# Retention and a GELU block on one Trainium2 core: the first block's second product by half-size products, and another order of loads

## The chip, the core and the metric

The kernel runs on one core of a Trainium2 chip. The core has a matrix engine (TensorE, "PE" in the profile; its weight loads are listed as PEld), a vector engine (VectorE, DVE), an engine for activation functions (ScalarE, ACT), a general engine (GpSimd, POOL) that here issues nearly all loads, and SyncE (SP), which here issues the stores. They run side by side, each its own instructions in order, and wait for each other by semaphores. On-chip data lies in SBUF; matrix products land in eight banks of PSUM.

The metric is the device time of one execution in microseconds. The kernel before took 288.04 us, the median of three runs (287.86 to 289.65).

## The reference

Inputs are q, k, v of shape (8, 8, 576, 64): 8 sequences, 8 heads, 576 positions, 64 features. The weights are w_in (512 x 2048) and w_out (2048 x 512).

```
gamma = 1.0 - 2.0 ** (-5.0 - arange(H))
Dmat  = where(rel >= 0, gamma ** rel, 0)        # rel = row position - column position
ret   = (scale * q @ k^T) * Dmat
x     = (ret @ v), heads put side by side        # (4608, 512)
h     = x @ w_in                                 # first product
out   = gelu_exact(h) @ w_out                    # second product, (4608, 512) float32
```

## The kernel before, in words

**Units, groups, blocks.** The 4608 rows are cut into 36 units of 128 tokens (a chunk of one sequence, or the 64-token tails of two). Units 0 to 3 are groups of their own; from unit 4 on a group is a pair of units (the same chunk of two sequences) or a tail. Four units make a block of 512 tokens, so there are nine blocks, t = 0 to 8. Group 4 (units 4, 5) and group 5 (units 6, 7) make block 1; groups 6 and 7 block 2.

**Attention of a group.** q and k are turned so that features lie on the partitions: by transposes on TensorE (`turn`, L515) for units 0 to 3 and for the groups in `BY_PE` (L73: groups 4 and 5), by block transposes on DVE (`turn_dve`, L541, with a rearranging copy on ACT, `apart`, L555) for all others. Then come the scores, a mask by DVE (`masked`), the products within the chunk (`inner`), the running state of a sequence pair (`state`, which for the DVE-turned groups needs k a second time in its natural order, the `kn_ld` load, item n in the list of loads) and the product with the state of the chunk before (`cross`). `evacuate` writes x to SBUF. Two neighbouring groups may be done in one go ("AA").

**The first product of a block** (`mlp1`, or `mlp1_fast` in the last blocks) multiplies x by w_in, 256 columns of w_in to a loaded chunk, in pieces of 128, 256 or 512 tokens, and ACT writes GELU of it to `g_all`. Block 0 is done chunk by chunk and unit by unit as both arrive. Block 1 is done by halves: units 4 and 5 for all chunks, then units 6 and 7.

**The second product** has two forms. The plain form (`mlp2`, L838) takes 16 matmuls of 512 columns for 128 tokens and needs of w_out only the rows that it multiplies. The form with seven half-size products (`mlp2_fast`, L904; a Strassen-Winograd scheme) does 256 tokens, p = 0 or 1, with 7 x 8 matmuls of 256 columns, instead of the 32 of 512 columns of the plain form for the same tokens. It needs sums of w_out, made once by DVE (`w_out_sums`, L861: eight instructions, in the order 1, 2, 4, 3, two each), and four sums of g per 256 tokens (`g_sum`, L875); partial results are copied out of PSUM (`snap`, by DVE or ACT) and joined by DVE (`join`, L900). The products are done in the order 1, 2, 6, 5, 7, 4, 3. Products 1 and 2 need w_out only, 6, 5, 7 and 4 its sums. `fast_ready` (L951) asks for all of w_out before any of them. Before the change blocks 1 to 8 use this form, and of block 0 the second half (p = 1); its first half is plain.

**What sets the order.** A planner in the kernel itself writes the instruction streams. It keeps an estimated time for each engine (`T`), picks for TensorE the next piece that is ready by the estimates, hands out DVE and ACT jobs in `side_jobs` and `fire`, and issues loads on POOL in the order of a list written by hand (`ORDER`, L376; items wi and wo are chunks of w_in and w_out, q, k, v and n those of a unit or pair, dq is a table, io the constants). On the chip each engine goes through its stream in that order. The constants at L85 to L104 steer the planner: AHEAD and RATE limit how far scores run ahead of the blocks, STATE10 holds back the first state of sequence pair 1, JOIN, VISIT, LEAD and NEAR decide when two groups are done in one go, SB how late DVE may be when scores are begun, PER_G and PER_B weigh DVE's jobs, MSK_AT says when the mask is due. The planner lets the sums of w_out start when by its estimate all of w_out has landed (L1233) and units 0 to 3 are through, as they use the space of those units' q and k. Block 2's first product may not begin before block 0's second is done, since they share `g_all`.

## Time and profile before

| | us |
|---|---|
| median of three runs | 288.04 |
| the profiled execution | 288.46 |
| its span (first to last instruction) | 286.7 |
| TensorE busy | 277.8 |
| DVE busy | 229.7 |
| ACT busy | 176.7 |
| POOL busy (issuing loads, mostly) | 141.0 |
| bytes moved by DMA | 31.97 MB |

The profile lists one execution. Busy time is the time in which an engine has an instruction running; matmuls overlap in the pipeline, so the time that a row of them takes is better read from the starts of one piece and the next. L450 is the line of a helper through which all matmuls go, and L454 of the one for transposes on TensorE, so pieces are told apart by their tiles: `x,w_in` is the first product, `w_out,g_all`, `wt,s`, `wt,g_all` and `w_out,s` the second, `q_ld,kT` the scores, `zeros` are dummy matmuls that only keep TensorE occupied. POOL's DMA instructions are the issuing; "to landing" counts from there to the arrival.

### The profile page before, as it was taken

The numbers are of one execution on the slowest core, as the hardware profiler recorded it, in microseconds if no ns is written. First come the engines' busy times: TensorE is split into PE (matmuls) and PEld (weight loads), VectorE is DVE, ScalarE is ACT, GpSimd is POOL, SyncE is SP. The second block draws the span as 40 slices with busy tenths as digits, with TensorE's granted clock in tenths as the row PEclk, the third lists the DMA queues.
The fourth block names the chain that finished last, engine by engine and source line by source line (L and its number), as shares of the span: only waits on it lengthen the run. The fifth ranks groups of instructions, "written<-read, shape, count | busy, mean of one in ns | idle before, by whom it ended". The sixth has DMA issues, their size and how long they took to land.

```text
span 286.7 us, 9851 instructions
## 1 busy us (share of the span) xinstructions
PE 277.8 (97%) x4216; PEld 210.3 (73%) x4216; DVE 229.7 (80%) x387; ACT 176.7 (62%) x403; POOL 141.0 (49%) x213
## 2 busy tenths in 40 slices
PE   7889998999999999999999999999999999999994
PEld 2568766888864657756676676677888888888883
DVE  6754586767995699898978599969999999999861
ACT  7456425876888895688587766764555363655421
POOL 8976898799959977778665864000000000000000
PEclk9999999999999999999999999999999999999999
DMA  9999999999999999999999996302020201202014
GB/s 158 176 179 188 195 152 173 188 132 143 128 154 108 116 167 120 205 146 135 142 150 160 101 139 54 71 2 75 2 75 0 77 4 72 75 0 75 37 57 129
DMA packets 109276, 31.97 MB, mean 112 GB/s; under 512 B 85936, under 2 KB 104880, under 8 KB 109232
## 3 DMA queue, kind: packets, MB, share of 16 engines
q0 software_dynamic: 100528, 21.12, 83.8%
q1 hardware_dynamic: 6752, 9.37, 9.9%
q10 hardware_dynamic: 1952, 0.85, 1.3%
q8 instruction: 33, 0.54, 0.8%
q14 instruction: 11, 0.09, 0.1%
HBM read 42.99 MB, written 9.44 MB: 183 GB/s over the span
## 4 chain that ended last, share of the span: by engine, by line
PE 61%; DMA 22%; POOL 12%; issue 2%; ACT 1%; DVE 0%; POOLq 0%
PE psum L450 60%; DMA kn_ld<-in_k_dram 6%; DMA w_out<-in_moe_w_out_dram 6%; DMA q_ld<-in_q_dram 5%; POOL k_ld L346 3%; POOL q_ld L346 2%; DMA v_ld<-in_v_dram 2%; DMA early<-in_q_dram 2%; POOL v_ld L357 2%; DMA k_ld<-in_k_dram 1%; POOL dqT L320 1%; PE psum L454 1%; POOL kn_ld L352 1%; POOL w_in L310 1%; POOL k_ld L336 1%
## 5 line engine op out<-in xcount | busy, mean ns | idle before, releaser
L450 PE MATMUL psum<-x,w_in 128*128 128x256 bf16 (+2 forms) x792 | 117.8, 295 | 0.6 <-DMA w_in<-in_moe_w_in_dram 0.6
L450 PEld LDWEIGHTS <-w_in 128*128 128x128 bf16 x792 | 69.0, 98 | 29.1 <-DMA w_in<-in_moe_w_in_dram 1.2
L450 PEld LDWEIGHTS <-g_all 128*128 128x128 bf16 x576 | 55.5, 98 | 13.5 <-issue 0.3
L450 PE MATMUL psum<-w_out,g_all 128*128 128x256 bf16 (+1 forms) x440 | 57.9, 280 | 0.0
L346 POOL DMA_DIRECT2D k_ld<-in_k_dram x64 | 35.5, 577 | 23.8 <-DMA kn_ld<-in_k_dram 14.1
L816 ACT ACTIVATE g_all<-psum 128x512 bf16<-128x512 f32 x64 | 36.9, 592 | 16.4 <-PE psum L450 14.8
L450 PEld LDWEIGHTS <-s 128*128 128x128 bf16 x408 | 39.5, 98 | 7.6 <-issue 0.6
L634 ACT ACTIVATE vh<-v_ld,dv 128x128 bf16<-128x128 bf16 (+1 forms) x144 | 42.1, 378 | 0.0
L617 DVE TENSOR_TENSOR ret<-psum,msk 128x1024 bf16<-128x1024 f32 (+1 forms) x32 | 35.5, 1149 | 6.3 <-PE psum L450 6.2
L1030 ACT ACTIVATE g_all<-t 128x512 bf16<-128x512 f32 x36 | 22.6, 630 | 28.2 <-DVE t L1038 28.2
L487 ACT COPY t<-psum 128x256 f32<-128x256 f32 (+1 forms) x48 | 20.7, 433 | 29.7 <-PE psum L450 29.5
L346 POOL DMA_DIRECT2D q_ld<-in_q_dram x64 | 35.6, 583 | 1.9 <-DMA k_ld<-in_k_dram 1.0
L450 PE MATMUL psum<-wt,s 128*128 128x256 bf16 x272 | 33.5, 273 | 0.3 <-ACT t L487 0.3
L901 DVE TENSOR_TENSOR o_sb<-psum,t 128x256 f32<-128x256 f32 x51 | 21.4, 420 | 13.1 <-PE psum L450 7.2
L1038 DVE TENSOR_TENSOR t<-psum,t 128x512 f32<-128x512 f32 x36 | 24.6, 687 | 2.7 <-ACT t L487 1.1
L819 ACT ACTIVATE g_all<-psum 128x256 bf16<-128x256 f32 (+1 forms) x43 | 19.5, 488 | 11.2 <-PE psum L450 10.6
L485 DVE COPY t<-psum 128x512 f32<-128x512 f32 (+1 forms) x39 | 21.6, 564 | 0.4 <-PE psum L450 0.3
L450 PE MATMUL psum<-x,ws 128*128 128x256 bf16 x144 | 19.5, 273 | 0.0
L450 PE MATMUL psum<-wt,g_all 128*128 128x256 bf16 x136 | 17.5, 273 | 0.0
L450 PE MATMUL psum<-w_out,s 128*128 128x256 bf16 x136 | 17.5, 273 | 0.0
L357 POOL DMA_DIRECT2D v_ld<-in_v_dram x14 | 16.5, 1180 | 1.0 <-ACT g_all L816 0.7
L785 DVE TENSOR_TENSOR x<-psum,dqT 128x1024 bf16<-128x1024 f32 (+1 forms) x14 | 15.5, 1137 | 0.1
(100 smaller groups left out, 326.2 us busy)
## 6 DMA issues: line engine op xcount, KB each, us to landing
out_dram<-o_sb SPq DMA_DIRECT2D x31, 256.0 KB, 3.3
q_ld<-in_q_dram POOLq DMA_DIRECT2D x56, 64.0 KB, 5.5
k_ld<-in_k_dram POOLq DMA_DIRECT2D x56, 64.0 KB, 4.7
v_ld<-in_v_dram POOLq DMA_DIRECT2D x14, 256.0 KB, 5.3
kn_ld<-in_k_dram POOLq DMA_DIRECT2D x12, 256.0 KB, 6.8
w_in<-in_moe_w_in_dram POOLq DMA_DIRECT2D x8, 256.0 KB, 8.4
w_out<-in_moe_w_out_dram POOLq DMA_DIRECT2D x8, 256.0 KB, 7.1
q_ld<-in_q_dram POOLq DMA_DIRECT2D x16, 32.0 KB, 4.5
```

The source lines that it names most:

```text
L346: nc.gpsimd.dma_start(qk["qk".index(what)][p0:p0 + 32, 0:HP * per].rearrange("p (h x) -> p h x", h=HP), {"q": q, "k": k}[what][2 * bp + jj ...
L357: nc.gpsimd.dma_start(v_ld.rearrange("p j h d -> p (j h) d"), v[2 * bp:2 * bp + 2, :, ci * C:ci * C + C, :].rearrange("b h s d -> s (b h) d"))
L450: nc.tensor.matmul(*a, **k)
L485: nc.vector.tensor_copy(dst, src)
L487: nc.scalar.copy(dst, src)
L617: nc.vector.tensor_tensor(both.rearrange("p (e h) s -> p e h s", e=2), t, by, op=ALU.mult)
L634: nc.scalar.activation(vh[:, 0:m, h], src[:, :, h], AF.Copy, scale=dv[:, h, ci:ci + 1])
L816: nc.scalar.activation(g_all[:, t % 2, :, m0, :], hT.rearrange("p n (a c) -> p (n a) c", a=2), AF.Gelu)
L819: nc.scalar.activation(g_of(t, 2 * lo // TOK)[:, m0:m0 + n, lo_:lo_ + hi - lo], hT, AF.Gelu)
L901: nc.vector.tensor_tensor(dst, src, f[key], op=ALU.add)
L1030: nc.scalar.activation(g_of(t, part)[:, m0:m0 + 2], src, AF.Gelu)
L1038: nc.vector.tensor_tensor(f[key], f["b"][1], f[key], op=ALU.add)
```

## The change

The second half of block 0 was already done by seven half-size products; now the first half is too, so no plain second product is left in the kernel. `sum_due`, the list of the sums of g, gets the four sums of block 0's first half. NPE goes from 2 to 1: group 5 is turned by DVE, as all groups behind it are, and therefore item n6 becomes a real load. The list of loads is reordered, and the planner's constants are set anew.

```diff
@@ -67,7 +67,7 @@
     PLAIN = 4
-    NPE = 2
+    NPE = 1
...
-    AHEAD = 35
-    RATE = 0.4
+    AHEAD = 27
+    RATE = 1.6
     STORE_AT = 62.0
     CROWD = 66.0
-    STATE10 = 28.0
+    STATE10 = -20.0
...
-    JOIN = 1
+    JOIN = 2
     JOIN_SB = 0.0
-    VISIT = 8
-    LEAD = -3.0
-    NEAR = 3.2
-    SLACK, SB, PER_G, PER_B, TURN0 = 1.2, 2.0, 8.0, 20.0, 0.0
+    VISIT = 6
+    LEAD = 5.0
+    NEAR = 1.4
+    SLACK = 1.2
+    SB = 2.6
+    PER_G = 6.0
+    PER_B = 20.0
+    TURN0 = 0.0
...
-    MSK_AT = -58.0
+    MSK_AT = -18.0
...
-    ORDER = ("wi4 io wo2 q2 q1 k1 k2 wi5 wi3 n4 v1 wi1 v2 wi0 wi2 k3 q3 v3 wi7 dq2 wi6 wo6 q4 wo4 q5 wo0 wo1 wo3 "
-             "wo5 k5 wo7 q6 k4 k7 v4 q7 k6 q8 v6 q12 dq0 q9 v12 k9 k13 q10 n8 k11 k8 v8 dq3 k10 q11 v10 k12 n10 "
-             "dq4 q13 n6 n12").split()
+    ORDER = ("wi5 io k1 q1 v2 v4 q3 v1 k3 q2 k2 v3 k4 wi1 q4 wi7 q5 wi0 wi2 k5 wi3 dq2 wi6 wo4 wi4 wo2 wo0 q6 wo3 "
+             "wo6 wo1 wo5 wo7 k6 n12 k8 v8 q7 q9 n4 n8 k7 k9 v6 dq3 n6 q10 k11 v12 k10 q8 q11 dq0 v10 dq4 q13 k12 "
+             "q12 k13 n10").split()
...
@@ -1102,8 +1106,8 @@
         elif t == 0:
-            runs2.append((t, [("2", t, ts, m, m + 2) for m in range(0, N_DF, 2) for ts in range(2)]))
-            runs2.append((t, [("f", t, 1, x) for x in "1265743"]))
+            for p in range(2):
+                runs2.append((t, [("f", t, p, x) for x in "1265743"]))
...
     for t in (0, *FAST2):
-        for p in range(2) if t else (1,):
+        for p in range(2):
             sum_due += [(t, p, i) for i in "1234"]
```

## The prediction

> **What bounds the kernel now.** I read the page first: its busy times, its slices and the shares of the chain of work that ended last.

> ```profile
> span 286.7 us, 9851 instructions
> PE 277.8 (97%) x4216; PEld 210.3 (73%) x4216; DVE 229.7 (80%) x387; ACT 176.7 (62%) x403; POOL 141.0 (49%) x213
> ...
> PEclk9999999999999999999999999999999999999999
> ...
> PE 61%; DMA 22%; POOL 12%; issue 2%; ACT 1%; DVE 0%; POOLq 0%
> ```

> TensorE is busy for 97% of the span, but a third of the chain is DMA and POOL. The view by stretches shows where, once without a filter (columns: stretch, its length, busy time and count per engine, granted clock, DMA share, GB/s) and once for the matmuls on the tile `zeros`, dummies that only keep TensorE occupied:

> ```profile
> 0.00:20.14 20.14, 16.57 (x209) 9.39 (x209) 14.28 (x47) 11.53 (x24) 17.05 (x26) 1.00 1.50 172
> 20.14:45.94 25.80, 24.71 (x337) 18.86 (x338) 15.33 (x24) 12.29 (x33) 21.33 (x29) 1.00 1.72 184
> 45.94:81.19 35.25, 35.19 (x744) 30.09 (x745) 27.21 (x36) 26.63 (x65) 30.34 (x46) 1.00 1.57 149
> 81.19:200.00 118.81, 118.43 (x2058) 78.10 (x2055) 98.62 (x141) 87.03 (x212) 72.28 (x113) 1.00 1.11 119
> 200.00:283.00 83.00, 82.94 (x873) 73.82 (x872) 73.84 (x142) 39.26 (x72) 0.00 (x0) 1.00 0.13 46
> ...
> 0.00:10.00 10.00, 6.30 (x17) 1.95 (x17) 0.27 (x1) 1.00 1.22 161
> 10.00:20.14 10.14, 2.34 (x7) 0.64 (x7) 0.00 (x0) 1.00 1.78 182
> ```

> From 45.94 us to 283 TensorE idles 0.06 + 0.38 + 0.06 = 0.5 us. So the end is fixed by two numbers: how much matmul work there is, and how much of the time before 45.94 is lost. Useful work by then is 16.57 + 24.71 - 6.30 - 2.34 = 32.6 us; **lost are 13.3 us**, 12.2 before 20.14 and 1.1 behind it. DVE is busy 83% (98.62 / 118.81) and 89% later on, close, but its waits end nothing there.

> **The change part by part.** First the matmul work, from the order of instructions on TensorE (start, duration, instruction; consecutive starts give the time a piece takes, since durations overlap):

> ```profile
> 33.01 8.12 PE L450 MATMUL psum<-w_out,g_all 128*128 128x512 bf16 x40
> 40.97 0.61 PE L454 MATMUL psum<-ident,k_ld 128*128 128x128 bf16 x8
> ...
> 45.94 0.61 PE L454 MATMUL psum<-ident,q_ld 128*128 128x128 bf16 x8 [1.08 <-DMA q_ld<-in_q_dram]
> 46.38 1.04 PE L450 MATMUL psum<-w_out,g_all 128*128 128x256 bf16 x8
> 47.47 0.61 PE L454 MATMUL psum<-ident,k_ld 128*128 128x128 bf16 x8
> 48.01 0.63 PE L450 MATMUL psum<-ret,vh 128*32 128x128 bf16 x32
> ...
> 49.17 1.05 PE L450 MATMUL psum<-wt,g_all 128*128 128x256 bf16 x8
> ...
> 56.35 7.16 PE L450 MATMUL psum<-x,w_in 128*128 128x256 bf16 x64
> 63.44 0.63 PE L450 MATMUL psum<-q_ld,kT 32*128 32x128 bf16 x32
> 64.00 3.67 PE L450 MATMUL psum<-x,w_in 128*128 128x256 bf16 x32
> ...
> 68.76 1.92 PE L450 MATMUL psum<-w_out,g_all 128*128 128x256 bf16 x16
> 70.52 1.91 PE L450 MATMUL psum<-wt,s 128*128 128x256 bf16 x16
> ```

> *Seven products.* Sixteen half-size matmuls take 70.52 - 68.76 = 1.76, 0.11 each. The piece from 33.01 to 40.97 is the plain product of the first token half, 32 matmuls of 512 columns, and eight half-size ones (merged in one row): 7.96 - 8 x 0.11 = 7.08 for the 32. In their place come 7 x 8 x 0.11 = 6.16. **Gain 0.92.**

> *One group fewer on TensorE.* Group 5 (units 6 and 7) loses its 16 transposes: 46.38 - 45.94 = 0.44 and 48.01 - 47.47 = 0.54. **Gain 0.98.** The 1.08 of waiting before 45.94 is for the same group's q; it goes too, and I count it with the lost time below.

> *What the other engines get.* These groups carry it (busy us, mean ns):

> ```profile
> L548 DVE STREAM_TRANSPOSE kT<-k_ld 128x512 f32<-128x512 f32 x12 | 13.4, 1114 | 0.0
> L559 ACT COPY q_ld<-qT 128x1024 bf16<-128x1024 bf16 x12 | 12.5, 1042 | 0.0
> L901 DVE TENSOR_TENSOR o_sb<-psum,t 128x256 f32<-128x256 f32 x51 | 21.4, 420 | 13.1 <-PE psum L450 7.2 <-ACT t L487 5.0 <-issue 0.2
> L883 DVE TENSOR_TENSOR s<-s,g_all 128x1024 bf16<-128x1024 bf16 x17 | 11.7, 688 | 0.4
> L485 DVE COPY q_ld<-psum 128x1024 bf16<-128x1024 bf16 x2 | 1.4, 690 | 2.4 <-PE psum L454 2.4
> ```

> DVE gains four sums (2.75), three joins (1.26) and two transposes (2.2), and loses one copy of 0.69: about 5.5 us. ACT gains a 1.04 copy; the short evacuations that it gains and loses roughly cancel. The cover on DVE is the 8.0 us in which it is free between 45.94 and 81.19 and the 10.5 before that. If that cover were gone the 5.5 us would meet a stage at 83% and be paid partly.

> *Loads.* The new order has group 5's natural-order k (item n6, no load before because the transposed tile served both uses), one more 256 KB transfer, with fourteen items of the list behind it: late enough to stand behind what TensorE needs first. More important is what moves ahead: group 4's q, k and v now precede most of w_in, and w_out comes last.

> ```profile
> 1.25 0.89 POOL L310 DMA_DIRECT2D w_in<-in_moe_w_in_dram  x1 [0.80 <-POOLq L1433]
> ...
> 31.13 0.73 POOL L325 DMA_DIRECT2D w_out<-in_moe_w_out_dram  x1
> ...
> w_in<-in_moe_w_in_dram POOLq DMA_DIRECT2D x1, 256.0 KB, 6.1
> ...
> w_out<-in_moe_w_out_dram POOLq DMA_DIRECT2D x1, 256.0 KB, 7.1
> ...
> L368 POOL DMA_DIRECT2D early<-in_q_dram x3 | 2.7, 892 | 0.2 <-issue 0.2
> L336 POOL DMA_DIRECT2D q_ld<-in_q_dram x8 | 6.1, 769 | 2.4 <-DMA w_in<-in_moe_w_in_dram 1.8 <-issue 0.6
> L357 POOL DMA_DIRECT2D v_ld<-in_v_dram x14 | 16.5, 1180 | 1.0 <-ACT g_all L816 0.7 <-issue 0.2
> ```

> The first chunk lands at 1.25 + 6.1 = 7.35, the last w_out chunk at 31.13 + 7.1 = 38.2. Between them land 15 chunks of 256 KB and 12 tiles of 128 KB, 5376 KB in 30.9 us: 174 KB/us. In the changed order POOL issues, ahead of the second w_in chunk, the first chunk (0.8), two iotas (0.45), nine tiles (9 x 0.9), v4 (1.18) and k4 (2 x 0.77): it starts at about 13.3 and lands 6 to 7 us later, at 20. From there to the last w_in chunk are 2176 KB, 12.5 us (32.5), to the last w_out chunk 4096 KB, 23.5 us (**43.5, where 38.2 was**).

> *Lost time.* By 20 us TensorE can have done the attention of units 0 to 3 and their work with one w_in chunk. That is one unit's attention more than before and w_in matmuls of one chunk instead of several, so about the 7.9 us of before (16.57 - 8.64); unit 3's v is among the last to land, so I take 7.4, an estimate that may be off by 0.7 either way: 12.6 lost. From 20 to 43.5 it has seven chunks of block 0's first product (16 matmuls of 256 columns each, 7.09 / 64 = 0.111 apiece: 12.4), group 4 (transposes 0.98 as above, scores 64.00 - 63.44 = 0.56, the rest 49.17 - 48.01 = 1.16: 2.7) and, new as cover, the first half of block 1's first product (64 matmuls, 7.1): 22.2 of work for 23.5. Then the first block's second product waits for the w_out chunks and for the DVE sums of w_out, which the replaced plain product did not:

> ```profile
> 36.17 1.28 DVE L870 TENSOR_TENSOR wt<-w_out 128x1024 bf16<-128x1024 bf16 x2
> ...
> 40.18 1.29 DVE L870 TENSOR_TENSOR w_out<-w_out 128x1024 bf16<-128x1024 bf16 x2
> ```

> All eight sums took 41.47 - 36.17 = 5.3; the first two read only the first half of w_out and began before the last chunk was there, at 36.17 against 38.2. So the last sums stand between 47.2 (begun early again) and 48.8 (begun at 43.5). Until then TensorE has 7.4 + 22.2 + four of the seven products (3.5) = 33.1 of work: lost 14.1 to 15.7. If the order is better than my count and only the wait before 45.94 goes, it is 12.2. I take 14.1, nearest to the row that shows the sums begun ahead of the last chunk: **0.8 more lost than before**. Behind the waiting matmul stands everything on TensorE, since it runs in order, and behind it the evacuations of block 0 and the first stores.

> *After that.* Group 5's v lands some 12 us behind the last w_out chunk by POOL's issue times, about 55 (ten loads at 1.18); the second product of block 0 (14 x 0.88 = 12.3) and the first half of block 1's (6.2) fill TensorE until about 62. No hole there.

> *The other constants.* MSK_AT is negative before and after, so the mask is due at once in both. The limits for scores ahead, the joining of two groups, the early state of pair 1 only reorder instructions in stretches where TensorE idles 0.5 us of 237: nothing can be gained, up to 1 us lost or some mode changes saved; I take 0, with 1 us to each side.

> *Sum.* -0.92 - 0.98 + 0.8 = -1.1. The profiled execution took 288.46, 1.76 more than its span and 0.4 over the median 288.04; span 285.6, execution 287.4, **287.0 at the median's level**.

> [...] The longest hole in which TensorE did nothing was 1.2 us, at the start, and the clock was granted at 1.00 in every stretch above:

> ```profile
> PE psum L450 <- DVE zeros L150: 1.2, 1, 1.2
> PE psum L454 <- DMA q_ld<-in_q_dram: 1.1, 1, 1.1
> ```

> [...]

> **The rivals.**

> 1. *The start gets tighter and nothing new waits.* For it: the wait for group 5's q is gone and work that needs no w_out is pulled ahead. Against: w_in's second chunk lands at 20, and 7.4 us of work before it isn't more than 7.9. Lost 12.2: -1.9 - 1.1 = **285.0**.

> 2. *The second product takes the place of the plain one as a wait (slower).* Its place is TensorE between the end of block 0's first product, near 35, and the sums of w_out near 47. What hides it is the 7.1 us of block 1, which needs q4, q5, k4, k5, two transposes, scores, mask, cross product and evacuation before it. Each us of that cover that comes too late is a us lost. With none of it 287.0 + 7.1 = 294.1, with half 290.6; over 290.9 (1% slower) from 3.9 us on. For it: the chain is DMA and POOL in that stretch, and a plain product that could start chunk by chunk is gone. Against: the last of group 4's loads, k5, is ahead of the last three w_in chunks. I price it at **291**.

> 3. *DVE becomes the bound* between 81 and 200, if its 5.5 us of new work and another order of its jobs push mask and evacuation late: **289.5**. Against: its 20 us of free time there.

> [...]

> That the seven products are not done as said can be excluded by the matmul counts; that the retuned constants change nothing cannot, and is within the forecast.

> **How the numbers follow.** Forecast 287.0, from 285.2 to 289 by the ends above (lost 13.3, as before, to 15.7, and some 0.7 us either way for the reordering): 0.52. Rival 1: 0.16. Rival 2: 0.24, two thirds of it above 290.9. Rival 3: 0.05. Rival 4: 0.03. A measurement of this kernel tells about 1%, 2.9 us, from no change: 0.15 faster (below 285.16), 0.20 slower, 0.65 within. The range, 284.8 to 291.8, reaches over rival 1's middle and into rival 2; about one in ten is left on each side.

> **What would show it.** The plain matmuls of 512 columns on w_out gone (32) and 56 half-size ones in their place; 16 transposes of L454 fewer; k by natural order 13 times instead of 12. The first matmul on w_out near 43, not 33; before it, matmuls of block 1 on w_in. Useful work by some 47 us near 33. Stretches behind 60 us as full as now. The prediction is wrong if TensorE has holes of together over 4 us between 30 and 60, if it is held by DVE after 80, or if much less than 12 us is lost before 45.

## The result, and the profile after

The changed kernel takes **289.73 us** (median of 20 runs, 288.24 to 293.52) against 288.04 us (20 runs, 287.09 to 289.65): ratio **1.0053, interval 1.0039 to 1.0066**. It is half a percent slower; the forecast was 0.4% faster, 287.0 us. Here and below the median is of all runs, and the ratio leaves out those more than 1.5% above the fastest, two of the 20 here. The time lies in the range given, but the sign is wrong, and the 2.7 us between the two numbers are what the rest is about. The profiled execution took 289.73 us (before: 288.46), its span is 288.0 us (286.7), and the last matmul ends at 284.20 (282.95): all of the difference is on TensorE, the tail behind it is 3.8 us in both.

The page of the kernel after, its busy times, the slices of the granted clock and the chain that ended last. In the new file the lines of helpers stand four further down: L454 is now the line of the matmuls and L458 that of the transposes.

```profile
span 288.0 us, 9786 instructions
PE 278.4 (97%) x4164; PEld 211.6 (73%) x4166; DVE 232.9 (81%) x390; ACT 180.0 (63%) x404; POOL 140.6 (49%) x214
...
PEclk9899999999999999999999999999999999999999
...
PE 94%; DMA 2%; issue 1%; POOL 1%; DVE 0%; ACT 0%; POOLq 0%
```

DMA and POOL made a third of the chain before and make 3% of it now: it runs through TensorE nearly from the start, dummies included, so it no longer shows what the loads cost. TensorE is busy for longer (278.4 against 277.8 us, dummies included), and "issue", time in which the engine waited for nothing that the profile shows, is in the chain.

The stretches, with the columns as in the prediction, for all instructions:

```profile
0.00:20.14 20.14, 15.86 (x171) 8.19 (x174) 12.93 (x45) 10.78 (x21) 16.81 (x26) 0.92 1.84 155
0.00:45.94 45.94, 41.20 (x584) 29.70 (x587) 31.38 (x71) 28.14 (x58) 36.15 (x53) 0.96 1.66 172
45.94:81.19 35.25, 35.25 (x656) 30.36 (x655) 27.67 (x39) 23.79 (x62) 31.66 (x47) 1.00 1.52 167
81.19:200.00 118.81, 117.78 (x2159) 76.40 (x2158) 102.22 (x151) 87.02 (x211) 72.74 (x114) 1.00 1.13 119
200.00:283.00 83.00, 83.00 (x763) 74.34 (x761) 70.81 (x130) 41.05 (x75) 0.00 (x0) 1.00 0.12 41
```

and the same view for the dummies on `zeros` alone:

```profile
0.00:20.14 20.14, 9.88 (x27) 3.39 (x30) 0.27 (x1) 0.92 1.84 155
...
0.00:45.94 45.94, 10.31 (x28) 3.39 (x30) 0.27 (x1) 0.96 1.66 172
```

Useful by 45.94 are 41.20 - 10.31 = 30.9 us, so **15.05 us are lost** there, where 13.3 were: +1.75. By 20.14 it is 15.86 - 9.88 = 5.98 useful, 14.2 lost (12.2 before). Behind 45.94 TensorE now idles 118.81 - 117.78 = 1.03 us instead of 0.06 + 0.38 = 0.44: +0.6. (The prediction's 0.5 takes in 0.06 more, which lie behind the last matmul, at 282.95.) And all its useful work is 278.4 - 10.3 = 268.1 us against 277.8 - 8.6 = 269.2: -1.1. The three sum to +1.25, the time by which the last matmul comes later (284.20 against 282.95).

The order on TensorE at the two places that matter (start, duration, instruction, idle time before it and its releaser):

```profile
34.87 0.37 PE L454 MATMUL psum<-q_ld,u_sb 32*64 32x128 bf16 x24
35.70 0.26 PE L454 MATMUL psum<-q_ld,u_sb 32*64 32x128 bf16 x8 [0.46 <-issue]
35.90 8.93 PE L454 MATMUL psum<-x,w_in 128*128 128x256 bf16 x88
44.66 1.91 PE L454 MATMUL psum<-w_out,g_all 128*128 128x256 bf16 x16
...
81.03 0.94 PE L454 MATMUL psum<-wt,g_all 128*128 128x256 bf16 x7
82.46 0.27 PE L454 MATMUL psum<-wt,g_all 128*128 128x256 bf16 x1 [0.49 <-issue]
```

The first product on w_out starts at 44.66, right behind 88 matmuls on w_in, with nothing waited for. The two stops are of another kind: each cuts a run of equal matmuls on the same tiles in two, and the view names no operand that came late. The view of waits on TensorE counts them, with two more behind them (us in all, times, longest):

```profile
PE psum L458 <- DMA early<-in_q_dram: 1.5, 1, 1.5
PE psum L454 <- issue: 1.5, 4, 0.5
```

The view of before has no such "issue" line among its waits.

Taken by kind, from the time between the starts of consecutive pieces in that order, idle time left out, the useful work of TensorE is:

| us | before | after |
|---|---|---|
| turning group 5 and 4 (`ident,q_ld`, `ident,k_ld`) | 1.87 | 0.89 |
| second products | 112.38 | 111.87 |
| first products | 122.90 | 122.60 |
| scores, masked product, cross product, state | 30.35 | 30.72 |
| turning units 0 to 3 | 2.31 | 2.42 |

No matmul of 512 columns on w_out is left. The column falls by 1.3 us; the count by busy time above, 1.1, differs by the overlap of neighbours.

### The profile page after: what moved, and what is told of

Same layout as the page of the kernel before. It is cut to its first block, busy times and chain, and to the rows that moved or that the text cites. A ratio compares the mean times of both kernels' runs of the same rounds, so it can differ in the third digit from the quotient of the medians.

```text
span 288.0 us, 9786 instructions
## 1 busy us (share of the span) xinstructions
PE 278.4 (97%) x4164; PEld 211.6 (73%) x4166; DVE 232.9 (81%) x390; ACT 180.0 (63%) x404; POOL 140.6 (49%) x214
## 4 chain that ended last, share of the span: by engine, by line
PE 94%; DMA 2%; issue 1%; POOL 1%; DVE 0%; ACT 0%; POOLq 0%
PE psum L454 93%; DMA early<-in_q_dram 2%; PE psum L458 1%; POOL w_in L314 0%; POOL early L372 0%; ACT qkT L491 0%; DVE qkT L489 0%; DVE o_sb L905 0%; POOL val L190 0%; POOL pos L192 0%; POOLq L190 0%; POOLq L1437 0%
## 5 line engine op out<-in xcount | busy, mean ns | idle before, releaser
L454 PE MATMUL psum<-x,w_in 128*128 128x256 bf16 (+2 forms) x728 | 118.7, 308 | 0.1
L454 PEld LDWEIGHTS <-w_in 128*128 128x128 bf16 x728 | 68.3, 98 | 27.0
L454 PEld LDWEIGHTS <-g_all 128*128 128x128 bf16 x576 | 55.5, 98 | 10.7
L454 PE MATMUL psum<-w_out,g_all 128*128 128x256 bf16 x432 | 54.7, 273 | 0.0
L454 PEld LDWEIGHTS <-s 128*128 128x128 bf16 x432 | 41.7, 98 | 9.2 <-issue 0.8
L350 POOL DMA_DIRECT2D k_ld<-in_k_dram x68 | 37.5, 571 | 19.9 <-DMA kn_ld<-in_k_dram 12.0
L350 POOL DMA_DIRECT2D q_ld<-in_q_dram x68 | 37.4, 572 | 2.0 <-DMA kn_ld<-in_k_dram 1.1
L491 ACT COPY t<-psum 128x256 f32<-128x256 f32 (+1 forms) x52 | 22.3, 428 | 25.2 <-PE psum L454 24.3
L454 PE MATMUL psum<-wt,s 128*128 128x256 bf16 x288 | 35.9, 273 | 0.0
L905 DVE TENSOR_TENSOR o_sb<-psum,t 128x256 f32<-128x256 f32 x54 | 22.6, 419 | 15.9 <-ACT t L491 9.3
L823 ACT ACTIVATE g_all<-psum 128x512 bf16<-128x512 f32 (+1 forms) x35 | 18.9, 559 | 10.3 <-PE psum L454 10.3
L489 DVE COPY t<-psum 128x512 f32<-128x512 f32 (+1 forms) x38 | 21.4, 569 | 1.0 <-PE psum L454 1.0
L454 PE MATMUL psum<-x,ws 128*128 128x256 bf16 x144 | 19.5, 273 | 0.0
L454 PE MATMUL psum<-wt,g_all 128*128 128x256 bf16 x144 | 18.7, 273 | 0.5 <-issue 0.5
L454 PE MATMUL psum<-w_out,s 128*128 128x256 bf16 x144 | 18.5, 273 | 0.3 <-issue 0.3
L552 DVE STREAM_TRANSPOSE qT<-q_ld 128x512 f32<-128x512 f32 (+1 forms) x17 | 16.0, 944 | 1.9 <-DMA q_ld<-in_q_dram 1.9
L361 POOL DMA_DIRECT2D v_ld<-in_v_dram x14 | 16.5, 1178 | 2.0 <-ACT t L491 0.7
## 6 DMA issues: line engine op xcount, KB each, us to landing
out_dram<-o_sb SPq DMA_DIRECT2D x31, 256.0 KB, 2.3
v_ld<-in_v_dram POOLq DMA_DIRECT2D x14, 256.0 KB, 5.5
kn_ld<-in_k_dram POOLq DMA_DIRECT2D x13, 256.0 KB, 6.2
w_in<-in_moe_w_in_dram POOLq DMA_DIRECT2D x8, 256.0 KB, 5.8
w_out<-in_moe_w_out_dram POOLq DMA_DIRECT2D x8, 256.0 KB, 8.7
```

Of the source, the lines that this page charges most:

```text
L350: nc.gpsimd.dma_start(qk["qk".index(what)][p0:p0 + 32, 0:HP * per].rearrange("p (h x) -> p h x", h=HP), {"q": q, "k": k}[what][2 * bp + jj ...
L361: nc.gpsimd.dma_start(v_ld.rearrange("p j h d -> p (j h) d"), v[2 * bp:2 * bp + 2, :, ci * C:ci * C + C, :].rearrange("b h s d -> s (b h) d"))
L454: nc.tensor.matmul(*a, **k)
L489: nc.vector.tensor_copy(dst, src)
L491: nc.scalar.copy(dst, src)
L823: nc.scalar.activation(g_of(t, 2 * lo // TOK)[:, m0:m0 + n, lo_:lo_ + hi - lo], hT, AF.Gelu)
```

## The experiments

Two explanations stood against each other at the outset: the new list of loads makes the start worse, whatever is computed; DVE, with its new sums and transposes, is late somewhere. A third came up when the first four kernels had run (the seven products alone, one group fewer, the plain product back, group 5 back): TensorE stops at places that depend on the count of its instructions and not on their operands. All kernels compute the whole output; four of them change only the number or size of the dummies on `zeros`. Each ratio is against the kernel before, on the same chip.

**The seven products alone.** In the kernel before:

```diff
-            runs2.append((t, [("2", t, ts, m, m + 2) for m in range(0, N_DF, 2) for ts in range(2)]))
-            runs2.append((t, [("f", t, 1, x) for x in "1265743"]))
+            for p in range(2):
+                runs2.append((t, [("f", t, p, x) for x in "1265743"]))
...
-        for p in range(2) if t else (1,):
+        for p in range(2):
```

> The kernel before with the seven half-size products for both token halves of block 0, its old order of loads, constants and TensorE transposes kept. Theory S (the start of the new load order loses the time, the products themselves save 0.9): here the start is the old one, but w_out lands as before, at 38, and nothing of block 1 is loaded yet to cover the wait from 33 on: a hole of 4 to 6 us on TensorE between 33 and 42, time 291 to 293. Rival P (the products just save their matmuls): 287.1, no new hole.

295.76 us, ratio 1.0259 (1.0235 to 1.0284): slower than expected. The order on TensorE of this kernel:

```profile
32.97 1.05 PE L450 MATMUL psum<-x,w_in 128*128 128x128 bf16 x16 [1.27 <-ACT g_all L819]
...
38.99 0.38 PE L450 MATMUL psum<-w_out,g_all 128*128 128x256 bf16 x2 [1.57 <-DMA w_out<-in_moe_w_out_dram]
40.73 0.61 PE L454 MATMUL psum<-ident,k_ld 128*128 128x128 bf16 x8 [1.35 <-DMA k_ld<-in_k_dram]
...
44.70 0.63 PE L450 MATMUL psum<-q_ld,kT 32*128 32x128 bf16 x32 [1.62 <-DVE kT L485]
```

The product waits for w_out at 38.99, and the pieces called in to fill the time wait too, one of them for its own load and one for DVE. The stretch up to 45.94 has 35.15 us busy, 8.56 of them dummies: 19.35 lost, 6 us more than before. So the plain product chunk by chunk was indeed cover, as the second rival has it. With the new list and constants the seven products lose no more than a plain product does (15.05 us by 45.94, against 15.0 and 15.3 in two kernels below): there the wait finds other cover.

**One group fewer on TensorE alone.** In the kernel before `NPE = 1`, nothing else.

> The kernel before with group 5 turned by DVE instead of TensorE, all else old. Theory S: the 0.98 of transposes go, and the wait for group 5's q (1.08) moves off TensorE: 286.0 to 287.0. Rival D (DVE's transposes or the late second load of k hold TensorE): group 5's state waits for its natural-order k, which stands near the end of the old list; a hole before group 7's product with the state, near 77, and 288 to 290.

293.68 us, 1.019 (1.0164 to 1.0215); both expectations missed. The transposes are saved (0.89 us are left of 1.87), and up to 45.94 lost time even falls a little (12.5). It is given back behind that: TensorE idles there for 4.9 us instead of 0.4, and the tail after the last matmul is 5.0 us instead of 3.8. The view of waits on TensorE names DVE:

```profile
PE psum L450 <- DVE t L485: 2.3, 3, 1.1
PE psum L450 <- DVE x L785: 1.4, 2, 1.0
```

So with the old list and the old constants, which place DVE's jobs, the third rival is real. In the changed kernel no such wait is left.

**The list and the constants alone.** In the kernel before the new `ORDER` and the new planner constants; the plain product and `NPE = 2` stay.

```diff
-    AHEAD = 35
-    RATE = 0.4
+    AHEAD = 27
+    RATE = 1.6
...
-    ORDER = ("wi4 io wo2 q2 q1 k1 k2 wi5 wi3 n4 v1 wi1 v2 wi0 wi2 k3 q3 v3 wi7 dq2 wi6 wo6 q4 wo4 q5 wo0 wo1 wo3 "
+    ORDER = ("wi5 io k1 q1 v2 v4 q3 v1 k3 q2 k2 v3 k4 wi1 q4 wi7 q5 wi0 wi2 k5 wi3 dq2 wi6 wo4 wi4 wo2 wo0 q6 wo3 "
...
```

> The kernel before with the new list of loads and the new constants alone: first half of block 0 plain, group 5 on TensorE. Theory S (the new order pays some 2 us at the start, whatever the products): lost time by 46 us 14.3 to 15 as in the changed kernel and not 12.7 as before. Rival (the lost time comes from the seven products' own wait): 12.7 to 13.3. The time of the whole depends on where pieces of instructions end: 290 to 298 by theory F.

295.81 us, 1.0265 (1.0225 to 1.0304). The first stretch of this kernel, for all instructions,

```profile
0.00:45.94 45.94, 40.90 (x574) 27.92 (x575) 27.86 (x66) 26.55 (x55) 37.36 (x53) 1.00 1.72 173
```

and for the dummies:

```profile
0.00:45.94 45.94, 9.95 (x30) 3.04 (x30) 0.27 (x1) 1.00 1.72 173
```

45.94 - (40.90 - 9.95) = **15.0 us lost, as in the changed kernel, without either of its two edits**. The extra loss at the start comes with the list and the constants, and a kernel below, with the list and the old constants, has it too: it is that of the list. The rest of the 7.8 us over the kernel before lies later: behind 45.94 this kernel idles for 5.1 us, and its view of waits on TensorE has

```profile
PE psum L454 <- issue: 2.3, 4, 1.1
PE psum L454 <- ACT t L491: 1.8, 2, 1.2
PE psum L454 <- DVE ret L621: 1.4, 2, 1.2
```

**The plain product back.** In the changed kernel the plain second product for the first half of block 0, the reverse of the first diff.

> The changed kernel with the first half of block 0 done by the plain product again. Theory S: the loss stands before 20 us and is untouched; 0.92 of matmuls come back: 290.2 to 290.8. Rival W (the wait for w_out and its sums is what costs): TensorE has work earlier, 288 to 289.

291.2 us, 1.0106 (1.0081 to 1.013), 1.5 us over the changed kernel. By kind, the second products take 112.8 us here and 111.9 there: **0.93 us for the seven products**, as the prediction had it; the rest is a little more idle time. Lost by 45.94 are 15.3 us. From 11.7 to 15.2 us, where the profile of the changed kernel has half the clock (last section), the clock is granted in full here, so the loss is not the clock's.

**Group 5 back on TensorE.** In the changed kernel `NPE = 2`.

> The changed kernel with group 5 turned by TensorE again (its second load of k gone). Theory S: 0.98 of transposes come back, little else: 290.4 to 291.0. Rival D (DVE's load holds TensorE): 288.5 to 289.3.

297.7 us, 1.0295 (1.0254 to 1.0336): 8.0 us over the changed kernel by the medians and 7.0 by the ratios, where the transposes are worth 0.98; both expectations missed. TensorE's order in this kernel:

```profile
137.60 1.08 PE L454 MATMUL psum<-ret,vh 128*32 128x128 bf16 x64
138.50 0.70 PE L454 MATMUL psum<-vh,kn_ld 128*32 128x64 bf16 x64
139.13 0.76 PE L454 MATMUL psum<-q_ld,u_sb 32*64 32x128 bf16 x64
139.83 0.94 PE L454 MATMUL psum<-w_out,g_all 128*128 128x256 bf16 x7
144.60 2.10 PE L454 MATMUL psum<-w_out,g_all 128*128 128x256 bf16 x9 [3.84 <-issue]
```

Here is a stop of 3.84 us amid sixteen equal matmuls. What stands ahead of it are 192 small matmuls, with their weight loads 384 instructions, in 139.83 - 137.60 = 2.2 us. During the stop one packet of 16 KB is moved on the queue that the view of transfers calls "instruction" (queue, packets, MB, share); the whole execution of the changed kernel has 32 of them, and its matmuls and weight loads together are 4164 + 4166 = 8330 instructions, 32.5 times 256:

```profile
q8 instruction: 1, 0.02, 1.6%
```

I read "issue" from this as a wait of TensorE for its next instructions; that is an inference from counts and times, and no view states it. The places speak for it. A matmul and its weight load are two instructions; the counts of weight loads up to the four stops of the changed kernel (PEld, the second count in each row) are:

```profile
0.00:35.24 35.24, 30.95 (x476) 20.46 (x478) 21.00 (x55) 21.61 (x45) 29.46 (x43) 0.95 1.68 167
0.00:81.97 81.97, 77.22 (x1243) 60.61 (x1246) 59.83 (x110) 52.71 (x119) 67.81 (x100) 0.98 1.61 170
0.00:158.77 158.77, 153.53 (x2648) 108.91 (x2650) 124.76 (x194) 112.45 (x262) 129.13 (x195) 0.99 1.52 157
0.00:164.59 164.59, 159.13 (x2776) 112.54 (x2778) 130.05 (x203) 115.22 (x268) 133.43 (x202) 0.99 1.53 156
```

1246 - 478 = 6 x 128, 2778 - 2650 = 128; and 2650 - 1246 = 10.97 x 128, within the few records that a trace can lack. The stops stand on steps of 128 matmuls, 256 instructions. The kernel with `NPE = 2` stops at counts of 478, 1244, 2393 and 2777, though it does other work there. The traces of the two kernels and the fourteen variants here have 38 such stops of over 0.15 us. Every one stands 88 to 94 weight loads behind a multiple of 128, and every one ends 1.2 to 1.7 us after a packet of 16 KB has been moved on the instruction queue. In the changed kernel the packets ahead of the four stops are through at 34.48, 80.90, 157.50 and 163.54, and the matmuls go on at 35.70, 82.46, 158.98 and 164.90; in the stop of 3.84 us the packet is moved from 142.23 to 143.21, and the matmuls go on at 144.60.

**The same work, shifted.** That is tested by moving the count alone. In the kernel before, each of the ten dummies of 512 columns at the start becomes four of 128: 60 instructions more, ahead of everything else, the order of all other work unchanged on every engine.

```diff
-        mm(t, lhsT=zeros[:, :128], rhs=zeros, start=True, stop=True)
+        mm(t[:, :128], lhsT=zeros[:, :128], rhs=zeros[:, :128], start=True, stop=True); [nc.tensor.matmul(t[:, :128], lhsT=zeros[:, :128], rhs=zeros[:, :128], start=True, stop=True) for _ in range(3)]
```

> The kernel before, its order of work unchanged on every engine; only the ten dummy matmuls of 512 columns at the start are forty of 128 columns (about as long), so TensorE's stream has 60 instructions more ahead of the same work. Theory F (TensorE's instructions come by DMA in pieces of 256, and a piece that comes late stops it; the planner laid the work out for the old places of the pieces): holes that wait for nothing the profile names appear in mid-row, 60 instructions earlier in the work than a multiple of 256 allows now, 1 to 6 us in all, 289 to 294. Rival (those holes come from something in the work itself): no new hole, 288.0.

**298.05 us, 1.0324 (1.0287 to 1.0362): ten microseconds by the medians, nine by the ratio, for sixty instructions on dummies.** Its view of waits has

```profile
PE psum L450 <- issue: 8.0, 6, 3.1
```

and its order on TensorE, at the longest of the six,

```profile
97.03 0.73 PE L450 MATMUL psum<-q_ld,u_sb 32*64 32x128 bf16 x61
100.85 0.24 PE L450 MATMUL psum<-q_ld,u_sb 32*64 32x128 bf16 x3 [3.08 <-issue]
```

where the kernel before has

```profile
95.38 0.76 PE L450 MATMUL psum<-q_ld,u_sb 32*64 32x128 bf16 x64
```

64 equal matmuls run through in the one and stop behind the 61st in the other. The stretch behind the stop shows what follows:

```profile
100.85:120.00 19.15, 19.15 (x284) 10.90 (x285) 16.32 (x24) 12.61 (x32) 13.80 (x22) 0.91 1.46 142
```

The granted clock is 0.91 over 19.15 us, which by 0.09 x 19.15 is another 1.7 us lost, an estimate. The first stops come at counts of 732 and 860, 128 apart, others at 1627, 2138, 2522 and 3290: the steps are those of the changed kernel (478 + 2 x 128 = 734), though this one has the old order.

The same edit in the changed kernel:

> The changed kernel with the same shift by 60 instructions, its order of work unchanged. Theory F: the four holes after 956, 2492, 5300 and 5556 instructions move to the same counts and so to other work; the sum of holes changes, by 1 us or more up if the planner had placed them well, and 289 to 293. Rival: the holes stay at the same pieces of work (35, 82, 159 and 165 us) and the time at 289.7.

296.41 us, 1.0261 (1.0222 to 1.0301): 3.5 us of "issue", the longest stop 1.9 us, again with a lower clock behind it (0.994 over the span, as much as one step of 3.41 us at half). Two of its four stops stand at counts of the kernel without the shift, 1246 and 2778, and so at other work. Its profile is 5.5 us longer than that of the changed kernel: 2.4 us more idle time behind 45.94, 0.9 more lost before it, and 2.0 in which the same work took longer. So the time of neither kernel follows from its work alone: it depends on where its small matmuls fall on the steps, and the kernel before stands better there (no stop, against 1.5 us).

**A shift back.** Six of the ten dummies at the start left out, 12 instructions fewer, the planner's own count as before:

```diff
-        mm(t, lhsT=zeros[:, :128], rhs=zeros, start=True, stop=True)
+        count[0] += 2.004; (_ < 4) and nc.tensor.matmul(t, lhsT=zeros[:, :128], rhs=zeros, start=True, stop=True)
```

In the changed kernel:

> The changed kernel with six of the ten dummy matmuls at the very start left out and every other instruction in its old order: TensorE's stream is 12 instructions shorter ahead of the same work. Theory F: each piece of 256 now ends where the planner thought that it would (its holes lie 6 to 14 instructions early now), so the holes at 35, 82, 159 and 165 us, 1.5 us together, go or shrink below 0.5; 288.2 to 289.0. Rival (the holes stay with the work, or fewer dummies cost more at the start than the holes): 289.6 or more.

289.5 us, 1.004 (1.0018 to 1.0062). Two of the four stops kept their counts, 478 and 2650, and so lie six matmuls later in the work; the other two are gone, and one at 1757 is new (TensorE's order in this kernel):

```profile
35.83 0.24 PE L454 MATMUL psum<-q_ld,u_sb 32*64 32x128 bf16 x2 [0.67 <-issue]
...
108.17 0.23 PE L454 MATMUL psum<-q_ld,u_sb 32*64 32x64 bf16 x8 [0.27 <-issue]
...
159.41 0.41 PE L454 MATMUL psum<-vh,kn_ld 128*32 128x64 bf16 x30 [0.49 <-issue]
```

The first came behind 24 of 32 matmuls and comes now behind 30. Together they are 1.43 us, as much as the 1.47 before. Lost time at the start can't be compared here, because with six dummies fewer the matmuls run at half pace for longer: the dummies at 8 to 9.7 us still follow each other 0.43 us apart, those at 7.6 to 8.6 in the changed kernel 0.22.

In the kernel before:

> The kernel before with the same six dummies left out, all else in its old order. Theory F: before has no such hole; by the times at which its trace passes the counts, the pieces that would then be used up fastest end at 59, 146 and 169 us (4.8, 4.4 and 4.1 us after the piece before them, where 4.7 was the shortest): new holes there of up to 0.7 each, 288.0 to 289.3. So the same edit should help the one and not the other. Rival (the edit acts at the start alone): both move the same way by the same amount.

287.94 us, 0.9995 (0.9969 to 1.0022): one stop, 0.17 us at 59, nothing in the time.

**The planner's own picture of it.** The planner knows of these pieces: `place` (in the kernel before at L456) counts instructions in pieces of 256 and `FETCH` is the least time between two. Two kernels change that in the changed kernel, the first by `FETCH = 7.0`:

> The changed kernel with the planner told that a piece of instructions takes 7.0 us to come instead of 5.0, so that it keeps small matmuls away from the places where one piece ends. Theory F: the four holes in mid-row (1.5 us together) shrink or go, 288.3 to 289.3 if the new order costs nothing else. Rival: the holes stay, 289.7 or more.

301.43 us, 1.0413 (1.0364 to 1.0462). The stops are nearly gone, and in the order that the planner now makes TensorE waits for other engines (the profile is of an execution of 297.97 us; what most of the others lose beyond that is not shown):

```profile
PE psum L454 <- DVE ret L621: 2.4, 2, 1.5
PE psum L454 <- DVE x L789: 1.8, 2, 1.6
...
PE psum L454 <- issue: 0.3, 1, 0.3
```

The second corrects the count: `(n - 188.0)` for `(n - 194.0)` in `place`, and 2.008 for 2.004 instructions a matmul.

> The changed kernel with the planner's own count of instructions set to where the holes of the runs lie (188 instead of 194 at the start, 2.008 instead of 2.004 to a matmul), so that it lays out the whole order anew. Theory F: holes in mid-row below 1 us together. The rest of the order is another one, so waits for DVE and ACT may come in as they did with the other fetch time: 287.5 to 294. Rival (the holes don't follow the count): holes of 1.5 us or more.

295.48 us, 1.024 (1.019 to 1.0291). The profile is of the fastest execution, 292.67 us. In it the three later stops are gone, but the first is longer (1.08 us at 35.12), and behind 160 us there is a wait of 2.2 us for DVE. Each such edit makes the planner choose another order everywhere, and neither order is as good.

**The constants back.** The changed kernel with the planner constants of before (all but `ORDER` and `NPE`).

> The changed kernel with the planner's constants of before; loads, products and NPE as changed. Theory S: lost time by 46 us 14 to 15.5, as in the changed kernel, since the loads set it. Theory F: the order of the work behind 46 us differs, so the holes in mid-row lie elsewhere; the constants had been chosen with them, 291 to 298. Rival (the constants cost, and the old ones are better): 287 to 289.

299.15 us, 1.0387 (1.0335 to 1.044). 5.5 us of "issue" (one stop of 4.48 us), 1.8 and 1.0 for ACT, 1.1 for a w_in chunk; 15.2 us lost by 45.94, again that of the list. So with this list the constants, which the prediction took at nothing, decide on 9 us.

**What binds the start.** Two kernels ask whether a better list would have helped. In the changed kernel w_in's second chunk and v4 exchange places in `ORDER`:

> The changed kernel with two items of its list of loads exchanged: the second chunk of w_in goes ahead to the place of the v pair of group 4 (both 256 KB), and that v pair to the chunk's. Theory S (the start loses the time, because until 20 us only one chunk of w_in is there): up to 1.8 us of first-product work moves ahead of 20 us; useful work by 20 us 7.3 to 8 instead of 6.0, time 288.0 to 288.8. Rival (the start is not what costs): useful work by 46 us unchanged and 289.7.

295.74 us, 1.0255 (1.0224 to 1.0286), with stops of 5.7 us, where the changed kernel has 1.5. Useful by 20.14 are 7.2 us instead of 6.0, but by 45.94 only 31.1 instead of 30.9: two waits give it back.

```profile
22.72 1.05 PE L454 MATMUL psum<-x,w_in 128*128 128x256 bf16 x8 [1.08 <-DMA w_in<-in_moe_w_in_dram]
...
37.98 6.27 PE L454 MATMUL psum<-x,w_in 128*128 128x256 bf16 x56 [0.84 <-DVE x L789]
```

In the kernel before, POOL issues q7's two loads ahead of v4, and all other streams stay as they are:

```diff
-                nc.gpsimd.dma_start(dst[:, e], {"q": q, "k": k}[what][2 * bp + j, HP * e:HP * e + HP, ci * C:ci * C + C, :].rearrange("h s d -> s h d"))
+                if (what, i) != ("q", 7): nc.gpsimd.dma_start(dst[:, e], {"q": q, "k": k}[what][2 * bp + j, HP * e:HP * e + HP, ci * C:ci * C + C, :].rearrange("h s d -> s h d"))
...
+            if i == 4: [nc.gpsimd.dma_start(tiles_of(7)[0][0].rearrange("p (h e j d) -> p e h j d", h=HP, e=2, j=2)[:, e, :, 1], q[2 * units[7][0] + 1, HP * e:HP * e + HP, units[7][1] * C:units[7][1] * C + C, :].rearrange("h s d -> s h d")) for e in range(2)]
```

> The kernel before with one exchange on POOL and every other engine's stream untouched: the two loads of q for unit 7 are issued ahead of the v pair of group 4, so the wait of 1.08 us before 45.94 loses its cause. Theory L (after 46 us every microsecond of lost time shows at the end, one for one): the wait goes, some 0.3 us may come back where v comes later, 287.0 to 287.5. Rival (the time is refilled later, or another load ends the same wait): 287.8 to 288.3.

288.86 us, 1.0038 (1.0009 to 1.0068): slower than both expectations. The wait for q7 (1.08) is gone, and a longer one has its place:

```profile
47.86 0.61 PE L455 MATMUL psum<-ident,k_ld 128*128 128x128 bf16 x8 [1.63 <-DMA k_ld<-in_k_dram]
```

The two waits differ by 0.55 us, the last matmul comes 0.58 later, and the time 0.8. What is lost here is lost at the end, one for one, and in this kernel loads bind TensorE until nearly 50 us.

## Why the prediction was right or wrong

*What bounds the kernel: right.* Useful work and lost time of TensorE account for the later end of its last matmul to 0.1 us.

*Seven products, 0.92: right.* Measured against the plain product in the new order 0.93. Against the kernel before, the second products fell by 0.5 only: a half-size matmul takes on average 0.1110 us in the new order and 0.1107 in the old, over a thousand of them 0.3 us. What makes that is not shown.

*Group 5 off TensorE, 0.98: right*, to the hundredth, by kind.

*DVE, +5.5 hidden: right in its effect.* Busy rose by 3.2 us only: the new jobs came as counted, and some 3.4 us of other copies on DVE went, which the prediction did not see; ACT's busy time rose by 3.3 where 1 was counted. No wait for DVE lies behind 46 us. The runs show how little was to spare: in other orders nearly the same work costs waits of 2 to 5 us for DVE.

*Lost time, +0.8: mis-sized; it measured +1.75.* The second chunk of w_in was issued at 14.1 (13.3 predicted), but by 20 us 14.2 us are lost and not 12.6, because before that chunk there was less to do than the 7.4 us that I took: 6.0. The hole that I set later, for the sums of w_out, did not come. The sums were done where predicted (the last ended at 47.7), the first product began at 44.66, and the 88 matmuls on w_in filled the time. Two errors, in opposite directions; the upper end given, 15.7, holds the 15.05.

*The other constants, 0, up to 1 us either way: this step failed.* The argument was that reordering can gain nothing where TensorE hardly idles, and lose little. It can lose much: the order sets where the small matmuls fall on the steps of 256 instructions. Of the 1.47 us of stops, 0.46 lie in the start and are part of the 1.75; 1.0 lie behind 81 us and make the idle time there, in place of waits of 0.4 for operands. The +0.6 there is inside the 1 us that I gave; that is luck, since the nine kernels here in which the planner made yet another order took 3 to 13 us more than the kernel before. The shift by dummies brings such stops with the work unchanged, 8.0 us of them, five times those here. What a change of mode on TensorE costs, which the prediction sets against that loss, no run shows. The new order was also taken to leave the work itself as it was, and that cost 0.8 us more. I had the slack of each engine before me, and not that of the instruction stream, which no view lists unless it fails.

*The sum.* Predicted were -1.9 of work, +0.8 lost, 0 behind: -1.1. Measured are -1.1, +1.75 and +0.6: +1.25. The 2.35 between them are 0.95 at the start (0.46 of it the stop there), 0.6 behind it and 0.8 of work; of that the kinds show 0.4 in the second products, 0.4 in attention and 0.1 in the transposes of the start, less 0.3 in the first products, and the last 0.2 lies between the two ways of counting. What makes the same matmuls take longer is not shown. The 2.7 between the two medians is that and 0.4 more, by which the profiled execution of the kernel before lay above its median and that of the changed one did not.

*The rivals.* The first (tighter start) fell with the list. The second's mechanism is there, at 6 us, if the products come without the new list, and not in the change as made. The third needs another order. The fourth, given 0.03, put a lower clock on top of the second; the trace of the kernel before shows no drop between 5.9 and 285.8 us, so that was an estimate of mine. It did not happen as set, but in other kernels: in the stop of 3.84 us the granted clock falls to half (stretches of the kernel with `NPE = 2`):

```profile
140.39:143.80 3.41, 0.38 (x4) 0.09 (x1) 2.16 (x2) 0.00 (x0) 2.74 (x3) 1.00 0.87 110
143.80:150.62 6.82, 6.02 (x25) 3.69 (x26) 3.79 (x7) 4.47 (x13) 3.89 (x8) 0.50 1.71 142
```

The half clock lasts 6.82 us here, twice 3.41, behind a stretch of 3.41 us with 3.41 - 0.38 = 3.03 us of idle time. Stops of 3.08 and 1.85 us in the two shifted kernels were followed by half clock too.

*What stays open.* That the change would break even without the stops (289.7 - 1.5 = 288.2) is arithmetic and was not shown: every edit that moved the stops left others in their place or changed the order. Why a half-size matmul is slower by 0.3 ns is open too.

## What to carry to other kernels

A planned order is fitted to the instruction stream as well as to the engines: sixty instructions more on TensorE, on dummies, moved all that followed against the steps of 256 on which the 38 stops stand, and brought 8.0 us of stops where there were none. A kernel without stops may owe that to luck or to a search. So price "only the constants" by shifting the stream with a few dummies, and if that alone moves the time by more than the edit is worth, forecast the spread and not the sum. And where loads bind the start, a product that needs all of a weight costs what it displaced as cover (6 us here with the old list), though its own arithmetic is cheaper (by 0.93).

## What the runs showed of the hardware

In the traces of both kernels TensorE starts at half pace: ten dummies take 4.45 us at the start of the kernel before, 0.43 us each, and later ones follow each other 0.22 us apart. Full clock is on record from 5.9 us there and from 4.9 in the changed kernel, and the 1.00 that the prediction read from the stretches does not hold for the time before.

Later the half clock came in steps of 3.41 us. The changed kernel has one of them:

```profile
8.33:11.74 3.41, 1.61 (x34) 1.04 (x34) 2.13 (x4) 2.62 (x4) 3.41 (x5) 1.00 2.44 155
11.74:15.15 3.41, 3.37 (x16) 1.75 (x15) 1.69 (x3) 0.41 (x2) 2.23 (x4) 0.50 2.43 154
```

In the step before it TensorE idled 3.41 - 1.61 = 1.80 us, 1.55 of them in one wait for a load. In each of the sixteen traces the clock changed only at multiples of 3.41 us from where full clock began: in the changed kernel at 4.92, 11.74 (two steps), 15.15 (three) and 288.23 (83). Of the steps run at full clock between the start and the last matmul, the seven in which TensorE idled 1.80 to 3.03 us are followed by half clock (1.80 in the changed kernel, 3.03 in the one with `NPE = 2`), and none in which it idled 1.71 or less, such as this one of the kernel with the seven products alone:

```profile
36.11:39.52 3.41, 1.70 (x14) 1.05 (x11) 3.22 (x6) 0.50 (x2) 2.88 (x4) 1.00 1.81 144
39.52:42.93 3.41, 2.21 (x24) 1.95 (x24) 3.41 (x6) 0.37 (x1) 3.41 (x6) 1.00 1.73 111
```

So in these traces the half clock went with the idle time in one step and not with the length of one wait: the 1.55 us wait of the changed kernel was followed by it, the wait of 1.57 in the kernel with the seven products alone, which ended at 38.99, was not. In the changed kernel it costs little: of the 3.37 us at half clock 2.93 are dummies, and half of the remaining 0.44, some 0.2 us by this estimate, is lost. Eight other executions of it, with a mean granted clock of 1.000, took 288.24 to 289.95 us.
